# One DRAM array for q, k and v with two loads a tile, four attention tiles in memory, and four tiles' scores and values in the product banks

## The chip, the core and the metric

The kernel runs on one core of one Trainium2 chip. What counts is the device time of one execution in microseconds. The kernel before took 833.31 us in the median of three runs (833.04 to 835.87).

## The reference

Inputs are q, k and v of shape (4, 8, 576, 64) and the weights of two feed-forward layers. The attention is block-diagonal: each head's 576 tokens fall into nine chunks of 64, and a chunk attends only to itself. The result, as 2304 tokens by 512 features, passes two layers, 512 to 2048 to 512, everything in float32.

```python
scores = scale * np.matmul(q_c, k_c.transpose(0, 1, 2, 4, 3))   # chunks of 64 x 64
attn = softmax(scores)                                          # row maximum taken off first
out = np.matmul(attn, v_c)                                      # -> x: 2304 x 512
g = s * np.maximum(x @ w_in, 0.0) ** 2 + b                      # layer 1
x = g @ w_out
h = x @ w_in2                                                   # layer 2
g = np.maximum(h, 0.0) + np.log1p(np.exp(-np.abs(h)))
out = g @ w_out2
```

## The kernel before, in words

**Tiles.** Attention works in 18 tiles of 128 token rows by 512 columns. Two tiles, an even and an odd one, make a unit; three units make a group, the 384 columns of a large product. Every large product is made of three float32r matmuls of high and low parts, and each layer's first product goes by a seven-product (Strassen-like) scheme. So a finished tile is not merely copied: sums of its quarters are formed and each is split into a high and a low part (`even_forms`, `odd_forms`, with `split` at L505 and L514 and `sub` at L492).

**A tile's chain** (`attention`, L693). Scores on TensorE (PE) into a PSUM bank (L733); row maximum on VectorE (DVE, L747); for the first six tiles (`EARLY`) the maximum is scaled on DVE (L769) and ScalarE (ACT) takes eight exponentials that also sum (L757), for the others DVE subtracts (L779), ACT takes one exponential (L792) and DVE sums (L800); two small DVE operations give the reciprocal of the sum (L810, L811); POOL multiplies (L817); PE transposes (L833); ACT or DVE copies the transpose out (L350, L352); PE multiplies by v (L852, the values); then the forms. The chain's last PE step is called V, its scores sc, its transposes T, with the tile's number behind them: sc0, T0, V0 for the first tile.

**Memory and banks.** Tiles stand in three sets of places in memory, tile t in set t mod 3. Each has four loads: q (128 rows), two halves of k (64 rows each, to the two blocks of a zero-padded matrix) and v. q and k may be loaded again as soon as the scores of the set's old tile are through, v as soon as its values are. Scores, transposes and values share three PSUM banks `at`; five more, A (two) and S (three), belong to the large products. Each of the five is cleared once, at the very start, by a matmul of zeros (L1404).

**Weights.** The first layer's weights arrive as 8-byte numbers in loads of 512 KB and are converted by five DVE operations and one on ACT (`convert`: L400, L430, L444, L458, L472, and L417 on ACT). Then DVE, POOL and ACT form their sums and split them (`weights1`).

**The order.** `Work.order` is a planner that runs while the kernel is built: every piece of work has engines, an estimated cost, a due key, dependencies and places that it takes and gives back. It writes one fixed order for each engine; each engine then goes through its own list in that order, and an instruction that waits holds up all behind it. All loads and stores stand in one such list, that of SyncE (SP). Keys of the first tiles are `TILE0 + t * TILE1`, a tile's loads are due `LEAD_Q` earlier, and `W_KEY` gives the keys of the first two weight pieces.

Of the kernel before, what the change touches and what calls it, by code (L numbers as in the profile page):

```python
# [9 lines left out]
F32R = mybir.dt.float32r  # L10
# [8 lines left out]
P = 128  # L19
B, H, S, D = 4, 8, 576, 64  # L20
NT = B * S
DM = H * D
DFF = 2048
KK = DM // P
NP = H // 2
# [15 lines left out]

EARLY = 6


LEAD_F, LEAD_Q, LEAD_W, LEAD_G, LEAD_H, LEAD_X = 12.0, 12.0, 14.0, 10.0, 4.0, 16.0

TILE0, TILE1 = 0.0, 2.5
START = [28.0, 40.0, 56.0, 64.0, 84.0, 92.0, 100.0]
W_KEY = [1.0, 45.0]


A_AT = {4: 0, 1: 1, 2: 2, 5: 3, 6: 4, 7: 5, 3: 6}
# [4 lines left out]
XS = 2 * 7 * 2 * P  # L57
LAST = (NG - 1) * GROUP
AT_X2 = LAST * XS
AT_W1 = NU * XS  # L60
# [9 lines left out]
AT_T = AT_XO + NXO * DM  # L70
# [27 lines left out]
class Work:  # L98
# [31 lines left out]
    def order(self, places):  # L130
# [14 lines left out]
        def earliest(op, e):  # L145
            t = engine[e]
            for d in op.deps:
                t = max(t, d.end + (self.OTHER if d.on != e else 0 if e == "PE" else self.SAME))
            for d in op.after:
                t = max(t, d.start)  # L150
            for u in op.takes:
                t = max(t, min(free[u.kind].values(), default=float("inf")))
            return t

        for op in self.ops:
# [3 lines left out]
        while len(done) < len(self.ops):  # L159
# [10 lines left out]
            t, op, e = best  # L170
# [45 lines left out]
def block_attention_two_layers(  # L216
    ctx: ExitStack,
    tc: tile.TileContext,
    q: bass.AP,
    k: bass.AP,  # L220
    v: bass.AP,
    w1: bass.AP,
    w2: bass.AP,
    s: bass.AP,
# [465 lines left out]
    last_small = [[], [], [], []]  # L690
    held = {}

    def attention(t, key):  # L693
        u, odd = t // 2, t % 2
        a = AT_X2 + t % 3 * XS
        spans = {
            "q": (a, 512),
            "k": (a + 512, 1024),
            "aT": (a + 1536, 512),
            "v": (a + 2048, 512),  # L700
            "e": (a + 2560, 512),
        }
        of = lambda x: mem(*spans[x], 0)
        own = []
        sp = lambda *x: [spans[y] for y in x]
        loads = [
            load(key - LEAD_Q, lambda: of("q"), lambda: q[t], P * DM * 4, uses=own, w=sp("q"), after=turn.get("q", ()))
        ]
        turn["q"] = loads[:1]
        for hp in range(2):  # L710
            p0 = hp * D

            loads.append(
                load(
                    key - LEAD_Q,
                    lambda p0=p0, hp=hp: of("k")[p0 : p0 + D, hp * 512 : (hp + 1) * 512],
                    lambda p0=p0: k[t, p0 : p0 + D],
                    D * DM * 4,
                    after=loads[-1:],
                    w=[(spans["k"][0] + hp * 512, 512)],  # L720
                )
            )
        load_v = load(
            key - LEAD_Q + 0.5, lambda: of("v"), lambda: v[t], P * DM * 4, uses=own, w=sp("v"), after=loads[-1:]
        )
        sc, pt, px = Place("at"), Place("at"), Place("at")

        def scores(e):
            out_ = at(sc).rearrange("p (a b k) -> p a b k", a=NP, b=2)
            kb = of("k").rearrange("p (b a c k) -> p b a c k", b=2, a=NP, c=2)  # L730
# [10 lines left out]
        o1 = add({"PE": 1.07}, key, scores, loads, [sc], r=sp("q", "k"))  # L741
        mx, sm = small[t % 4] if tc else (None,) * 2
        heads = lambda x: x.rearrange("p (h k) -> p h k", h=H)
        o2 = add(
# [109 lines left out]
                        )  # L854

        key += 0.3
        o10 = add({"PE": 1.07}, key, values, [o9, load_v], [px], r=sp("aT", "v"))
        got = lambda: two(at(px))
        hold = u >= LAST
        if hold or not odd:  # L860
# [34 lines left out]
    def quad(ph, i, j, w, keys, kinds):  # L895
# [68 lines left out]
            hid_in.setdefault((ph, n, j), []).append(st)  # L964
            quads_done[ph].append(st)

        p1 = product(1, ba, free_from.get("s2", ()), True)
        sb = seed(bb, keys[6] - 1, [p1])
        p6 = product(6, ba, [sb])
        c2 = add(  # L970
# [171 lines left out]
    def second_by_blocks(ph, t0):  # L1142
# [166 lines left out]
                        )  # L1309

    scalars = [
        add({"SP": 0.63}, -3, lambda e: nc.sync.dma_start(out=s_sb, in_=s.to_broadcast([P, 1]))),
        add({"SP": 0.63}, -3, lambda e: nc.sync.dma_start(out=b_sb, in_=b.to_broadcast([P, 1]))),
    ]

    T = 6 * mm(N)
# [36 lines left out]
    times += [(t0, 1), (t0 + 7 * T, 1)]  # L1353
    for t in tiles:
        attention(t, x_key(t))
    another_use()
    for u in range(LAST, NU):
        forms_held(u, x_key(TILES - 1) + 3 + u - LAST)
# [34 lines left out]
    with tc.manual_schedule():  # L1393
        nc.scalar.preload_act_table_set("exp_and_others")
        make_identity(nc, ident)
        for x in range(AT_X2, AT_W1, XS):
            nc.gpsimd.memset(mem(x + 512, 512, 0)[D:P], 0.0)
            nc.gpsimd.memset(mem(x + 1024, 512, 0)[0:D], 0.0)

        zero, ones = mem(AT_T, 512), mem(0, 512).bitcast(F32R)  # L1400
        nc.vector.memset(zero, 0.0)
        nc.vector.tensor_copy(out=ones, in_=zero)
        for x in bank["A"] + bank["S"]:
            nc.tensor.matmul(x, ones[:, :P], ones, start=True, stop=True)  # L1404
        for op in done:
            op.emit(op.on)


_INS = ["q", "k", "v", "w1", "w2", "s", "b"]
_OUTS = [((DM, NT), "float32")]  # L1410


def _laid_out(q, k, v, moe_w_in, moe_w_out, moe_s, moe_b, moe2_w_in, moe2_w_out):
    import numpy as np

    nch = S // D

    def heads_on_rows(a):

        a = a.reshape(B, NP, 2, nch, D, D).transpose(0, 3, 2, 5, 1, 4)  # L1420
        a = a.reshape(TILES, 2, 2, D, NP, D).transpose(0, 2, 3, 4, 1, 5)
# [12 lines left out]
    return {  # L1434
        "q": heads_on_rows(q),
        "k": heads_on_rows(k),
        "v": tokens_on_rows(v),
        "w1": weights(moe_w_in, moe_w_out),
        "w2": weights(moe2_w_in, moe2_w_out),
        "s": moe_s,  # L1440
        "b": moe_b,
    }
# [30 lines left out]
```

## Time and profile before

| | |
|---|---|
| median of three runs | 833.31 us |
| the profiled execution | 836.06 us |
| its span, first to last instruction | 834.3 us |
| PE busy | 795.1 us (95%) |
| DVE busy | 654.0 us (78%) |
| ACT busy | 506.4 us (61%) |
| POOL busy | 148.6 us (18%) |
| DMA moved | 180.26 MB, mean 216 GB/s |

Shares of the whole span hide the stages. The first 100 us, where the attention runs, look quite different from the rest, so this profile is read by windows: how long each engine was busy in a stretch, and at which waits it stood still. A duration is that of a group of instructions that the trace merges: "x16" is one tile's scores, "x4" its transposes, "x32" one tile's values where the group ends within 2 us or less.

### The profile page before, as it was taken

The page shows a single profiled execution, that of the slowest core. Times are in us where ns is not written, and L with a number is a line of the kernel's source. Part 1 is how long each engine was busy: PE and PEld are TensorE (multiplying, and loading weights), DVE is VectorE, ACT ScalarE, POOL GpSimd, SP SyncE. Part 2 cuts the span into 40 slices and gives each one's busy share as a digit, 9 for nine tenths or more (in the row PEclk, how much of TensorE's full clock was granted, in tenths as well). Part 3 has the DMA queues.
Part 4 walks back from the last instruction along what each step waited for, and adds up shares of the span by engine and source line. Part 5 has one row for each costly group of instructions (what it writes and reads, how often), then busy time and mean ns, then how long its engine had stood idle before and what let it go on. Part 6 is the DMA issues. An engine that isn't in the chain of part 4 may idle for free.

```text
span 834.3 us, 14524 instructions
## 1 busy us (share of the span) xinstructions
PE 795.1 (95%) x5117; PEld 775.0 (93%) x5117; DVE 654.0 (78%) x1174; ACT 506.4 (61%) x1076; POOL 148.6 (18%) x162
## 2 busy tenths in 40 slices
PE   4688889999999999999999989999999999999998
PEld 3577789999998999999999989999999999999997
DVE  5799888888967869888888776778784767777865
ACT  3655555666656877767767655555555655555543
POOL 4254240111111003222213540111110000000000
PEclk9899999999999999999999999999999999999999
DMA  8665347868757835767662027657667996688851
GB/s 235 195 190 170 106 144 241 262 240 269 257 218 275 324 107 161 244 225 255 224 197 88 11 95 262 232 197 251 246 233 253 354 372 226 203 262 297 277 187 57
DMA packets 80632, 180.26 MB, mean 216 GB/s; under 512 B 9008, under 2 KB 53040, under 8 KB 79664
## 3 DMA queue, kind: packets, MB, share of 16 engines
q1 hardware_dynamic: 80560, 179.34, 63.9%
q8 instruction: 40, 0.66, 0.3%
q14 instruction: 32, 0.26, 0.1%
HBM read 111.15 MB, written 68.16 MB: 215 GB/s over the span
## 4 chain that ended last, share of the span: by engine, by line
PE 83%; DVE 8%; DMA 3%; ACT 3%; issue 1%; POOL 1%; SPq 0%; ACTq 0%; DVEq 0%
PE at L916 17%; PE S L916 10%; PE S L1093 9%; PE at L1093 9%; PE S L1244 8%; PE at L1244 8%; PE A L916 7%; PE A L1093 6%; PE A L1244 5%; DVE operands L514 2%; DVE mem L492 2%; PE at L852 2%; PE at L733 1%; DMA mem<-in_w_dram 1%; DMA last<-in_k_dram 1%
## 5 line engine op out<-in xcount | busy, mean ns | idle before, releaser
L492 POOL TENSOR_TENSOR mem<-mem 128x256 f32<-128x256 f32 x120 | 109.6, 923 | 414.1 <-DVE mem L472 309.2
L514 DVE TENSOR_TENSOR operands<-mem,operands 128x384 fp32r<-128x384 f32 (+4 forms) x186 | 130.9, 720 | 45.0 <-ACT operands L505 43.1
L505 ACT CAST operands<-mem 128x384 fp32r<-128x384 f32 (+4 forms) x186 | 112.3, 620 | 58.8 <-PE at L1244 36.1
L514 DVE TENSOR_TENSOR operands<-last,operands 128x384 fp32r<-128x384 f32 (+2 forms) x184 | 110.5, 616 | 42.4 <-ACT operands L505 39.9
L505 ACT CAST operands<-last 128x384 fp32r<-128x384 f32 (+2 forms) x184 | 94.3, 528 | 73.2 <-PE A L1093 46.5
L916 PE MATMUL at<-operands 128*128 128x384 f32 x624 | 122.4, 340 | 4.1 <-ACT mem L350 2.0
L916 PEld LDWEIGHTS at<-operands 128*128 128x128 f32 x624 | 110.4, 190 | 6.7 <-ACT mem L350 2.7
L1093 PE MATMUL S<-operands 128*128 128x384 f32 x432 | 90.7, 335 | 0.4 <-DVE operands L514 0.4
L1093 PE MATMUL at<-operands 128*128 128x384 f32 x432 | 90.3, 334 | 0.0
L1244 PE MATMUL S<-operands 128*128 128x384 f32 x384 | 87.4, 334 | 0.1
L1244 PE MATMUL at<-operands 128*128 128x384 f32 x384 | 87.1, 334 | 0.0
L916 PE MATMUL S<-operands 128*128 128x384 f32 x420 | 83.5, 337 | 0.9 <-DVE S L492 0.8
L1093 PEld LDWEIGHTS S<-operands 128*128 128x128 f32 x432 | 76.2, 188 | 0.9 <-DVE operands L514 0.6
L1093 PEld LDWEIGHTS at<-operands 128*128 128x128 f32 x432 | 76.2, 188 | 0.0
L948 ACT ACTIVATE mem<-S 128x384 f32<-128x384 f32 x104 | 50.6, 492 | 41.1 <-PE S L916 34.4
L916 PEld LDWEIGHTS S<-operands 128*128 128x128 f32 x420 | 73.5, 188 | 1.5 <-DVE S L492 1.3
L1244 PEld LDWEIGHTS S<-operands 128*128 128x128 f32 x384 | 68.3, 188 | 0.4 <-DVE operands L514 0.4
L1244 PEld LDWEIGHTS at<-operands 128*128 128x128 f32 x384 | 68.3, 188 | 0.0
L916 PE MATMUL at<-last,operands 128*128 128x384 f32 x336 | 67.2, 337 | 0.6 <-ACT S L938 0.2
L492 DVE TENSOR_TENSOR mem<-mem 128x384 f32<-128x384 f32 (+1 forms) x108 | 60.7, 589 | 9.1 <-ACT mem L948 7.8
L1093 PE MATMUL A<-operands 128*128 128x384 f32 x288 | 65.4, 334 | 0.0
L916 PE MATMUL A<-operands 128*128 128x384 f32 x300 | 60.5, 341 | 3.3 <-ACT S L938 1.5
(79 smaller groups left out, 1217.0 us busy)
## 6 DMA issues: line engine op xcount, KB each, us to landing
mem<-in_w_dram SPq DMA_DIRECT2D x64, 512.0 KB, 4.4
summed<-mem SPq DMA_DIRECT2D x168, 192.0 KB, 2.3
mem<-summed SPq DMA_DIRECT2D x30, 768.0 KB, 4.8
hid<-mem SPq DMA_DIRECT2D x96, 192.0 KB, 2.9
last<-hid SPq DMA_DIRECT2D x24, 768.0 KB, 5.3
last<-summed SPq DMA_DIRECT2D x12, 768.0 KB, 4.9
mem<-forms SPq DMA_DIRECT2D x7, 1024.0 KB, 7.1
last<-in_q_dram SPq DMA_DIRECT2D x18, 256.0 KB, 4.2
```

The source lines that it names most:

```text
L492: lambda e: on(e).tensor_tensor(out=out(), in0=x(), in1=y(), op=op or ALU.subtract),
L505: lambda e: nc.scalar.copy(out=hi().bitcast(F32R), in_=x()),
L514: lambda e: nc.vector.tensor_tensor(out=lo().bitcast(F32R), in0=x(), in1=hi(), op=ALU.subtract),
L733: nc.tensor.matmul(out_[c * D : (c + 1) * D, pr], of("q")[:, pr * P + c * D : pr * P + (c + 1) * D], kb[:, :, pr, c, :], start=True, stop= ...
L852: nc.tensor.matmul(at(px)[y, x], of("v")[y, x], of("aT")[y, x], start=True, stop=True)
L916: nc.tensor.matmul(acc(dst)().rearrange("p (u c) -> p u c", u=GROUP), l[a], r[c], start=start and kk == 0 and x == 0, stop=kk == 1 and x == 2,
L948: lambda e: nc.scalar.activation(out=at(go), in_=acc(place)(), func=AF.Softplus if ph else AF.Relu),
L1093: nc.tensor.matmul(at(accs[d])[:, :N], l[a], r[c], start=m == 0 and z == 0, stop=m == NM - 1 and z == 2,)
L1244: nc.tensor.matmul(at(accs[d])[:, :N], l[a], r[c], start=i == 0 and y == 0, stop=i == NF - 1 and y == 2,)
```

## The change

It has four parts.

1. q, k and v come from one DRAM array. A tile has two loads: rows 0 to 63 bring q, the first k block and v as one stretch of 1536 numbers a row, rows 64 to 127 bring the same three as 3 pieces of 512 numbers, because the second k block lies elsewhere in memory. Scores and values now both wait for both loads.
2. Tiles stand in four sets. The transposed exponentials (aT) take the place of q. Both loads of a tile wait until the values of the set's old tile are through.
3. The scores of tiles 0 to 3 go to the A banks and their values to the S banks. The five clearing matmuls move from the start to behind tile 3's last use of these banks (`prime`, L1368 of the changed kernel), and the large products wait for them.
4. Keys: the first weight piece is due at 6 instead of 1, the two loads of scalars s and b at 60 instead of -3. The planner counts several places of one kind that a piece of work takes together.

```diff
+EARLY_BANKS = 4
...
-W_KEY = [1.0, 45.0]
+W_KEY = [6.0, 45.0]
...
-        a = AT_X2 + t % 3 * XS
...
+        a = AT_X2 + t % 4 * 5 * DM
+        spans = {x: (a + y * DM, DM) for x, y in (("q", 0), ("k0", 1), ("v", 2), ("e", 3), ("k1", 4), ("aT", 0))}
...
-        loads = [
-            load(key - LEAD_Q, lambda: of("q"), lambda: q[t], P * DM * 4, uses=own, w=sp("q"), after=turn.get("q", ()))
-        ]
-        turn["q"] = loads[:1]
+        loads = []
         for hp in range(2):
-            p0 = hp * D
+
+            def three(hp=hp):
+                rows = mem(a, 5 * DM, 0)[hp * D : (hp + 1) * D].rearrange("p (n c) -> p n c", c=DM)
+                return rows[:, 0:5:2] if hp else rows[:, 0:3]
 
             loads.append(
                 load(
                     key - LEAD_Q,
-                    lambda p0=p0, hp=hp: of("k")[p0 : p0 + D, hp * 512 : (hp + 1) * 512],
-                    lambda p0=p0: k[t, p0 : p0 + D],
-                    D * DM * 4,
-                    after=loads[-1:],
...
+                    three,
+                    lambda hp=hp: qkv[t, hp * D : (hp + 1) * D],
+                    3 * D * DM * 4,
+                    after=loads[-1:] or turn.get("qkv", ()),
...
-        load_v = load(
-            key - LEAD_Q + 0.5, lambda: of("v"), lambda: v[t], P * DM * 4, uses=own, w=sp("v"), after=loads[-1:]
-        )
-        sc, pt, px = Place("at"), Place("at"), Place("at")
+        turn["qkv"] = loads[-1:]
+        sc, pt, px = Place("A" if t < EARLY_BANKS else "at"), Place("at"), Place("S" if t < EARLY_BANKS else "at")
...
-        o10 = add({"PE": 1.07}, key, values, [o9, load_v], [px], r=sp("aT", "v"))
+        o10 = add({"PE": 1.7}, key, values, [o9, *loads], [px], r=sp("aT", "v"))
+        if t < EARLY_BANKS:
+            early.extend([o1, o10])
...
-        p1 = product(1, ba, free_from.get("s2", ()), True)
+        p1 = product(1, ba, (*primed, *free_from.get("s2", ())), True)
...
-        add({"SP": 0.63}, -3, lambda e: nc.sync.dma_start(out=s_sb, in_=s.to_broadcast([P, 1]))),
-        add({"SP": 0.63}, -3, lambda e: nc.sync.dma_start(out=b_sb, in_=b.to_broadcast([P, 1]))),
+        add({"SP": 0.63}, 60, lambda e: nc.sync.dma_start(out=s_sb, in_=s.to_broadcast([P, 1]))),
+        add({"SP": 0.63}, 60, lambda e: nc.sync.dma_start(out=b_sb, in_=b.to_broadcast([P, 1]))),
...
+        if t == EARLY_BANKS - 1:
+
+            places = [Place(kind) for kind in "AASSS"]
+
+            def prime(e):
+                for p in places:
+                    nc.tensor.matmul(at(p), ones()[:, :P], ones(), start=True, stop=True)
+
+            primed.append(add({"PE": 1.2}, x_key(t) + 0.7, prime, early, places, r=[ONES]))
...
-        for x in range(AT_X2, AT_W1, XS):
-            nc.gpsimd.memset(mem(x + 512, 512, 0)[D:P], 0.0)
-            nc.gpsimd.memset(mem(x + 1024, 512, 0)[0:D], 0.0)
...
+        for x in range(AT_X2, AT_X2 + 4 * 5 * DM, 5 * DM):
+            nc.gpsimd.memset(mem(x + DM, DM, 0)[D:P], 0.0)
+            nc.gpsimd.memset(mem(x + 4 * DM, DM, 0)[0:D], 0.0)
...
-        for x in bank["A"] + bank["S"]:
-            nc.tensor.matmul(x, ones[:, :P], ones, start=True, stop=True)
...
+    q, k, v = heads_on_rows(q), heads_on_rows(k), tokens_on_rows(v)
+    qkv = np.stack([q, k, v], axis=2)
+    qkv[:, D:] = np.stack([q, v, k], axis=2)[:, D:]
```

**How the order moves.** SP's list began with tile 0's four loads, then two weight loads, then q, k, v of tile 1 and of tile 2. It now begins with the two loads of tiles 0, 1 and 2, then the two weight loads, then tile 3, then s and b, then tile 4.

The DVE list begins, before, with the following; L400 to L472 convert the first weight piece, L747 is the maximum of tile 0 and L810, L811 its reciprocal:

```order
L747 TENSOR_REDUCE mx_76<-at_70 128x8
L400 TENSOR_SCALAR mem<-mem 128x512
L769 TENSOR_SCALAR mx_76<-mx_76 128x8
L430 TENSOR_SCALAR mem<-mem 128x512
L444 SCALAR_TENSOR_TENSOR mem<-mem 128x512
L458 SCALAR_TENSOR_TENSOR mem<-mem 128x512
L472 SCALAR_TENSOR_TENSOR mem<-mem 128x512
L400 TENSOR_SCALAR mem<-mem 128x512
L430 TENSOR_SCALAR mem<-mem 128x512
L810 TENSOR_SCALAR sm_77<-sm_77 128x8
L811 RECIPROCAL sm_77<-sm_77 128x8
```

With the change it begins so (L751 is what L747 was, L402 what L400 was, L814 and L815 what L810 and L811 were):

```order
L751 TENSOR_REDUCE mx_76<-A_65 128x8
L773 TENSOR_SCALAR mx_76<-mx_76 128x8
L751 TENSOR_REDUCE mx_78<-A_66 128x8
L402 TENSOR_SCALAR mem<-mem 128x512
L814 TENSOR_SCALAR sm_77<-sm_77 128x8
L815 RECIPROCAL sm_77<-sm_77 128x8
L773 TENSOR_SCALAR mx_78<-mx_78 128x8
L432 TENSOR_SCALAR mem<-mem 128x512
```

The maxima of tiles 0 and 1 now stand ahead of the first weight conversion, which stands ahead of tile 0's reciprocal.

The PE list, before, behind the five clearing matmuls:

```order
L733 MATMUL at_70<-last_120 64x128 x8
L733 MATMUL at_71<-last_120 64x128 x8
L733 MATMUL at_72<-last_120 64x128 x8
L833 MATMUL at_70<-ident,last_120 128x128 x4
L852 MATMUL at_70<-last_120 64x64 x16
L733 MATMUL at_71<-last_120 64x128 x8
L733 MATMUL at_70<-last_120 64x128 x8
L833 MATMUL at_72<-ident,last_120 128x128 x4
L852 MATMUL at_72<-last_120 64x64 x16
```

And with the change, from its start (L737 are scores, L837 transposes, L856 values):

```order
L737 MATMUL A_65<-last_120 64x128 x8
L737 MATMUL A_66<-last_120 64x128 x8
L737 MATMUL A_65<-last_120 64x128 x8
L837 MATMUL at_70<-ident,last_120 128x128 x4
L737 MATMUL A_66<-last_120 64x128 x8
L856 MATMUL S_67<-last_120 64x64 x16
L837 MATMUL at_71<-ident,last_120 128x128 x4
L856 MATMUL S_68<-last_120 64x64 x16
L837 MATMUL at_72<-ident,last_120 128x128 x4
L737 MATMUL at_70<-last_120 64x128 x8
L856 MATMUL S_69<-last_120 64x64 x16
```

Tile 1's transposes and values now follow tile 0's at once; before, the scores of tiles 3 and 4 stood between.

The third place is the clearing's new one on PE, between the values of tile 4 and the transposes of tile 5; the scores in the last row are tile 7's:

```order
L856 MATMUL at_71<-last_120 64x64 x16
L1368 MATMUL A_65<-operands 128x512
L1368 MATMUL A_66<-operands 128x512
L1368 MATMUL S_68<-operands 128x512
L1368 MATMUL S_69<-operands 128x512
L1368 MATMUL S_67<-operands 128x512
L837 MATMUL at_70<-ident,last_120 128x128 x4
L737 MATMUL at_72<-last_120 64x128 x8
```

Thirteen large products of the first layer stand ahead of the last tile's values in both orders.

## Rows read from the trace of the kernel before

**Rows 1.** Windows: us, busy time (instructions) by engine, granted clock, DMA share, GB/s.

```profile
core 0: us, PE busy (x) PEld busy (x) DVE busy (x) ACT busy (x) POOL busy (x), PEclk, DMA share, GB/s
0.00:10.00 10.00, 4.47 (x21) 3.09 (x21) 3.87 (x8) 2.91 (x10) 4.02 (x12) 1.00 0.77 242
10.00:20.00 10.00, 5.00 (x36) 3.93 (x36) 7.86 (x15) 5.14 (x28) 4.34 (x5) 1.00 1.00 230
20.00:30.00 10.00, 7.64 (x100) 6.68 (x100) 5.42 (x14) 6.28 (x34) 2.10 (x2) 0.92 0.63 179
30.00:40.00 10.00, 5.20 (x78) 4.24 (x74) 8.39 (x16) 5.61 (x26) 3.51 (x4) 0.84 0.72 230
40.00:50.00 10.00, 8.66 (x122) 7.17 (x120) 8.46 (x17) 6.23 (x20) 3.47 (x4) 0.73 0.41 128
50.00:100.00 50.00, 43.32 (x658) 37.68 (x660) 46.37 (x91) 27.63 (x51) 22.26 (x23) 1.00 0.49 150
100.00:140.00 40.00, 36.96 (x220) 34.80 (x215) 35.85 (x59) 25.45 (x53) 9.44 (x10) 1.00 0.56 189
140.00:834.00 694.00, 683.83 (x3900) 677.43 (x3898) 537.80 (x959) 427.15 (x861) 99.47 (x102) 1.00 0.65 223
```

**Rows 2.** Waits of DVE from 0 to 100 us: total us, times, longest.

```profile
DVE mx L747 <- PE at L733: 7.5, 3, 5.1
DVE mem L492 <- PE at L852: 2.9, 2, 2.1
DVE mem L352 <- PE at L852: 2.0, 1, 2.0
```

**Rows 3.** Timeline of DVE: start, duration, instruction, idle time before it and its releaser.

```profile
7.32 0.69 DVE L747 TENSOR_REDUCE mx<-at 128x8 f32<-128x512 f32 x1 [5.14 <-PE at L733]
...
8.26 0.16 DVE L769 TENSOR_SCALAR mx<-mx 128x8 f32<-128x8 f32 x1
```

**Rows 4.** Timeline of PE in the first 101 us.

```profile
2.23 1.22 PE L1404 MATMUL A<-operands 128*128 128x512 f32 x2 [2.23 <-DVE operands L1402]
3.25 1.48 PE L1404 MATMUL S<-operands 128*128 128x512 f32 x3
5.31 1.97 PE L733 MATMUL at<-last 128*64 128x128 f32 x16 [0.57 <-DMA last<-in_k_dram]
12.46 1.98 PE L733 MATMUL at<-last 128*64 128x128 f32 x16 [5.18 <-DMA last<-in_k_dram]
...
17.76 1.12 PE L833 MATMUL at<-ident,last 128*128 128x128 f32 x4
20.08 1.97 PE L852 MATMUL at<-last 64*64 64x64 f32 x32 [1.20 <-DVE last L352]
...
48.81 0.63 PE L833 MATMUL at<-ident,last 128*128 128x128 f32 x4
50.12 1.15 PE L852 MATMUL at<-last 64*64 64x64 f32 x32 [0.67 <-ACT last L350]
...
99.39 1.15 PE L852 MATMUL at<-last 64*64 64x64 f32 x32
```

**Rows 5.** DMA traffic of 0:3, 3:6, 6:9, 9:12, 30:33 and 674:684 us.

```profile
DMA packets 171, 0.32 MB, mean 107 GB/s; under 512 B 15, under 2 KB 15, under 8 KB 171
DMA packets 377, 0.88 MB, mean 292 GB/s; under 512 B 49, under 2 KB 49, under 8 KB 377
DMA packets 379, 0.99 MB, mean 330 GB/s; under 512 B 51, under 2 KB 51, under 8 KB 379
DMA packets 396, 0.70 MB, mean 234 GB/s; under 512 B 54, under 2 KB 54, under 8 KB 396
DMA packets 338, 1.01 MB, mean 337 GB/s; under 512 B 39, under 2 KB 39, under 8 KB 338
DMA packets 742, 4.26 MB, mean 426 GB/s; under 512 B 80, under 2 KB 80, under 8 KB 647
```

**Rows 6.** DMA issues of 684:700 us: number, size, us to landing.

```profile
mem<-summed SPq DMA_DIRECT2D x4, 768.0 KB, 4.4
```

More of the change, by code (lines that the diff above doesn't have):

```diff
@@ L150, in earliest @@
                 t = max(t, d.start)
-            for u in op.takes:
-                t = max(t, min(free[u.kind].values(), default=float("inf")))
+            kinds = [u.kind for u in op.takes]
+            for z, kind in enumerate(kinds):
+                times, n = sorted(free[kind].values()), kinds[:z].count(kind)
+                t = max(t, times[n] if n < len(times) else float("inf"))
             return t
@@ L218, in block_attention_two_layers @@
     tc: tile.TileContext,
-    q: bass.AP,
-    k: bass.AP,
-    v: bass.AP,
+    qkv: bass.AP,
     w1: bass.AP,
@@ L691, in block_attention_two_layers @@
     held = {}
+    early, primed = [], []
+    ONES = (5 * XS, 512)
+    ones = lambda: mem(*ONES).bitcast(F32R)
     def attention(t, key):
         u, odd = t // 2, t % 2
-        a = AT_X2 + t % 3 * XS
[L696 to L702, printed above, removed]
+        a = AT_X2 + t % 4 * 5 * DM
+        spans = {x: (a + y * DM, DM) for x, y in (("q", 0), ("k0", 1), ("v", 2), ("e", 3), ("k1", 4), ("aT", 0))}
         of = lambda x: mem(*spans[x], 0)
@@ L715, in attention @@
                     key - LEAD_Q,
-                    lambda p0=p0, hp=hp: of("k")[p0 : p0 + D, hp * 512 : (hp + 1) * 512],
-                    lambda p0=p0: k[t, p0 : p0 + D],
-                    D * DM * 4,
-                    after=loads[-1:],
-                    w=[(spans["k"][0] + hp * 512, 512)],
-                )
-            )
-        load_v = load(
-            key - LEAD_Q + 0.5, lambda: of("v"), lambda: v[t], P * DM * 4, uses=own, w=sp("v"), after=loads[-1:]
-        )
-        sc, pt, px = Place("at"), Place("at"), Place("at")
+                    three,
+                    lambda hp=hp: qkv[t, hp * D : (hp + 1) * D],
+                    3 * D * DM * 4,
+                    after=loads[-1:] or turn.get("qkv", ()),
+                    w=[spans["k1"], (a, DM // 2), (a + 2 * DM, DM // 2)]
+                    if hp
+                    else [spans["k0"], (a + DM // 2, DM // 2), (a + 2 * DM + DM // 2, DM // 2)],
+                )
+            )
+        turn["qkv"] = loads[-1:]
+        sc, pt, px = Place("A" if t < EARLY_BANKS else "at"), Place("at"), Place("S" if t < EARLY_BANKS else "at")
         def scores(e):
             out_ = at(sc).rearrange("p (a b k) -> p a b k", a=NP, b=2)
-            kb = of("k").rearrange("p (b a c k) -> p b a c k", b=2, a=NP, c=2)
+            kb = mem(a + DM, 4 * DM, 0).rearrange("p (n a c k) -> p n a c k", n=4, a=NP, c=2)[:, 0:4:3]
             for pr in range(NP):
@@ L739, in scores @@
                     )
-        o1 = add({"PE": 1.07}, key, scores, loads, [sc], r=sp("q", "k"))
+        o1 = add({"PE": 1.7}, key, scores, loads, [sc], r=sp("q", "k0", "k1"))
         mx, sm = small[t % 4] if tc else (None,) * 2
@@ L1395, in block_attention_two_layers @@
         make_identity(nc, ident)
-        for x in range(AT_X2, AT_W1, XS):
-            nc.gpsimd.memset(mem(x + 512, 512, 0)[D:P], 0.0)
-            nc.gpsimd.memset(mem(x + 1024, 512, 0)[0:D], 0.0)
-        zero, ones = mem(AT_T, 512), mem(0, 512).bitcast(F32R)
+        for x in range(AT_X2, AT_X2 + 4 * 5 * DM, 5 * DM):
+            nc.gpsimd.memset(mem(x + DM, DM, 0)[D:P], 0.0)
+            nc.gpsimd.memset(mem(x + 4 * DM, DM, 0)[0:D], 0.0)
+        zero = mem(AT_T, 512)
         nc.vector.memset(zero, 0.0)
-        nc.vector.tensor_copy(out=ones, in_=zero)
-        for x in bank["A"] + bank["S"]:
-            nc.tensor.matmul(x, ones[:, :P], ones, start=True, stop=True)
+        nc.vector.tensor_copy(out=ones(), in_=zero)
         for op in done:
             op.emit(op.on)
-_INS = ["q", "k", "v", "w1", "w2", "s", "b"]
+_INS = ["qkv", "w1", "w2", "s", "b"]
 _OUTS = [((DM, NT), "float32")]
@@ L1434, in _laid_out @@
     return {
-        "q": heads_on_rows(q),
-        "k": heads_on_rows(k),
-        "v": tokens_on_rows(v),
+        "qkv": qkv,
         "w1": weights(moe_w_in, moe_w_out),
```

## The prediction

> **What bounds the kernel now.** I read the windows first [rows 1]. Behind 140 us PE is busy 683.83 of 694 us: there the time is the large products, which the change leaves alone. From 100 to 140 us PE stands 3.04 us. In the first 100 us it is busy only 4.47 + 5.00 + 7.64 + 5.20 + 8.66 + 43.32 = 74.3, so 25.7 us stand open, nearly all of what a change can win. What the products wait for there is the attention: its last values begin at 99.39 [rows 4]. And what sets the attention's pace is DVE. From 50 to 100 us DVE is busy 46.37 of 50; from 0 to 50 only 3.87 + 7.86 + 5.42 + 8.39 + 8.46 = 34.0, so it stands 16.0 us [rows 1]. The waits say for what [rows 2]: for scores 7.5 us, 5.1 of them once, at the start, and for values (L852) 2.9 and 2.0. Behind the scores stand the loads: PE stood 5.18 us until tile 1's k had landed at 12.46 [rows 4]. Meanwhile DVE converted weights, so it looks busy, while tile 1 had not begun. Then PE's list held V0 back until 20.08, and values five tiles on (V5) began at 50.12.
>
> So the measure is simple: DVE's work up to the attention's end is the same in both kernels (no DVE instruction is added or removed), and what its idle time shrinks by, the end comes earlier, if PE can follow. Half a per cent, about what a measurement can tell from no change, is 4.2 us.
>
> **The loads.** A tile is 2 x 64 rows x 6 KB = 0.786 MB. Rows of 2 KB moved at 234 GB/s (9 to 12 us: 342 packets above 512 B for 0.70 MB, 2 KB each), a mix of weight rows of 4 KB and v at 337, and rows of 6 to 8 KB at 426 [rows 5]. I take 426 for the first load of a tile, whose rows are 6 KB at both ends (0.92 us), and 234 for the second, whose rows fall into three pieces in memory (1.68): 2.6 us a tile; 512 KB of weights at 337, 1.56. How long after its last byte a load counts as landed: by the traffic summed up [rows 5], tile 0's q and k (0.524 MB) were through at 3.7 and its scores began at 5.31 [rows 4], 1.6 later; all up to tile 1's k (2.36 MB) at 9.7 and its scores at 12.46, 2.7 later. These are my two ends.
>
> With 1.6: by 3.0 us 0.32 MB have moved, as before; tile 0 is through at 4.85 and lands at 6.45, 1.1 later than now since it holds v too; tile 1 lands at 9.05 (now 12.46), tile 2 at 11.65, the first weights at 13.2, tile 3 behind the second weights at 17.4. With 2.7, those behind tile 0 land 1.1 later.
>
> [...]
>
> **DVE's idle time after the change, up to V5.**
> - Start, until the clearing source is written: 0.9, as before.
> - Until tile 0's maximum: scores take 1.97 [rows 4], so 6.45 + 1.97 = 8.42; DVE is free at 7.32 - 5.14 = 2.2 [rows 3], so 6.25. Now it is 5.14: 1.1 worse.
> - Until tile 1's maximum: tile 0's takes 0.69 and the scaling 0.16 [rows 3], DVE is free at 9.3; tile 1's scores run 9.05 to 11.0: 1.75, new. Weight conversion filled this time before.
> - The conversion's first operation then stands ahead of tile 0's reciprocal and waits for the weights, 11.75 to 13.2: 1.45, new.
> - From there DVE has several tiles' work in its list. V0 stands behind tile 3's scores: 17.4 + 1.97 = 19.4 (now 20.08). Behind V0 come T1 and the copy of its result, for which DVE waits about 0.45, and one gap of 0.1, if PE's steps behind V1 go at the pace they had at 48 us and later: transposes 0.63, values 1.15 [rows 4]. That is 0.55. The waits of 2.0, 2.0 and 2.1 for scores and values [rows 2] go, since tiles 1 to 3 have their exponentials before V0 is through, and V1 follows V0 at once.
>
> Sum 10.9, against 16.0 now. Ahead of V5 both lists hold about the same work for DVE (two weight conversions and most of a third, the forms of tiles 0 to 4, the maxima of a few tiles more), 34 us; so V5 is 5.1 us ahead. With 2.7 for landing, tile 1's wait is 2.85 and the sum 12.0: 4.0 ahead. I take the middle, **4.5**.
>
> **The other edits.** The five clearing matmuls cost 1.22 + 1.48 = 2.7 [rows 4] where PE waited for tile 0 anyway, so taking them away there wins nothing. At their new place, with PE at the later pace, about half of that, 1.35, stand between V4 and T5. Tile 5's multiply on POOL is due some 0.7 us after V4, so PE is 0.65 late, and DVE has tile 5's and tile 6's rows to go on with: nothing. At the slow pace 2.7: 2.0 late, and tile 7's maximum, for which PE must first do T5, finds DVE empty for about 1.7. The first product waits for the clearing too, but it began at 57 and the clearing is done by about 45: nothing. 36 loads fewer: SP issues them while it waits for PE, nothing. The keys of s and b move little: they still stand right behind tile 3. Two more memsets on POOL end about 1.1 us later, ahead of any work there. The first weights' conversion ends some 5 us later, and nothing needs them before 57.
>
> **Does the lead last?** From 50 to 100 us DVE is busy 93% [rows 1], and V5 to V17 takes 49.3 us [rows 4], 4.1 a tile. Nothing in that stretch waits for what the change takes away, so the lead passes to the last values, now at 99.39, then near 95, and, as the products ahead of it are as many, to the end. The products' own waits may move by a us either way, as every list behind is written anew.
>
> Sum: the profiled execution took 836.06 us (span 834.3, 1.8 around it), the median is 2.75 lower. 836.06 - 4.5 = 831.6 as this execution counts, and 833.31 - 4.5 = **828.8** against the median.
>
> **Rivals.**
> 1. *The lead melts on PE's pace.* From 5 to 22 us a tile's scores or values took 1.97 us, at 50 us and later values 1.15; the granted clock was 0.73 to 0.92 from 20 to 50 us and 1.00 later [rows 1, 4] (the slow early rows stand under a recorded 1.00, so I go by durations). If PE stays slow up to V5, the copies that wait for T1, V2, T3 and T4 stand 2.1 us instead of 0.55, and the clearing costs its 1.7: the lead is 4.5 - 3.25 = 1.25, 832.1. Against it: with the change PE's steps from tile 3's scores on lie close together, where now it stands 5 of the 10 us from 30 to 40. Chance 0.3.
> 2. *Slower: the sets of memory bind.* A tile's loads now wait for the values four tiles back, where q and k waited only for scores three back. The new list puts a tile's scores mostly one values-step, 4.1 us, and one transpose, 0.63, behind the values that free its set. A load of 768 KB in gaps landed 4.4 us after its issue [rows 6], and there is a second issue: about 4.9, against 4.7. That is a tie, which DVE's list covers. If tiles land at 5.5, each of the twelve from 6 to 17 stands 0.8 us, 9.6 in all, and the time is 833.31 - 4.5 + 9.6 = 838.4. It turns the sign from 5.1 us (12 x 0.4). For it speaks that weights and stores share the DMA engines; against it that they are 0.49 busy from 50 to 100 us [rows 1]. Chance 0.12.
> 3. *More.* If the second load too runs at 426 GB/s, a tile takes 1.85 us, tile 1 lands 1.5 and the weights 2.25 earlier; the third and fourth item shrink by about 2.2: 826.6. Chance 0.12.
>
> The forecast itself has 0.46.
>
> **The numbers.** The forecast reaches from 4.0 to 5.1 us of lead, and with a us for the products' waits from 3.0 to 6.1: 827.2 to 830.3. The range takes in rival 3 and rival 1 with a little over a us beyond each: 825.3 to 833.5; it leaves out rival 2. Faster by over half a per cent (below 829.1): rival 3 and 0.38 of the forecast, 0.50. Within it: rival 1 and 0.08, 0.38. Slower: 0.12.
>
> **What would show it.** Right: tile 0's scores at 6.5, tile 1's near 9.6, V0 near 19.5, V5 near 45.6, the last values near 95; DVE idle in the first 45 us about 11.5. Wrong: DVE waiting for scores with a tile's load as the cause behind 50 us (rival 2); scores and values still at 1.97 between 25 and 45 us (rival 1); V5 ahead but the last values not, which would break the step that the lead lasts.

## The result, and the profile after

The changed kernel takes **844.33 us** in the median of four runs (841.48 to 844.87), the kernel before 834.09 in the same comparison (833.04 to 835.87): ratio 1.0124, interval 1.0095 to 1.0153. I had forecast 828.8, at most 833.5. It is some 10 us slower, and outside the range. The profiled spans are 843.0 and 834.3 us, so 8.7 us of it can be read in the two traces. The ratios of the runs below leave out one execution of run 2, which took 1576 us where its other nine took 833 to 838.

The windows of the changed kernel, columns as in [rows 1]:

```profile
0.00:10.00 10.00, 1.98 (x16) 1.60 (x16) 2.07 (x4) 1.28 (x1) 5.05 (x14) 1.00 0.82 184
10.00:20.00 10.00, 5.07 (x36) 3.92 (x36) 5.39 (x12) 6.38 (x35) 1.93 (x2) 1.00 0.94 235
20.00:30.00 10.00, 6.27 (x88) 5.24 (x88) 9.71 (x19) 5.78 (x24) 5.72 (x7) 1.00 0.48 114
...
50.00:100.00 50.00, 40.23 (x612) 33.85 (x608) 47.53 (x91) 28.33 (x50) 23.70 (x25) 1.00 0.75 183
100.00:140.00 40.00, 36.97 (x249) 34.69 (x250) 27.30 (x48) 24.74 (x50) 7.62 (x9) 0.96 0.44 143
140.00:834.00 694.00, 686.42 (x3910) 679.15 (x3909) 535.83 (x955) 433.53 (x872) 94.61 (x102) 1.00 0.65 225
```

The first 10 us already differ: DMA is as busy as before (0.82 against 0.77) but moves 184 GB/s instead of 242. And from 50 to 100 us DVE is busy for 47.53 us against 46.37, yet PE for 40.23 against 43.32: DVE works more, and PE gets less from it.

The PE timeline of the changed kernel shows where the attention stands (L737 scores, L837 transposes, L856 values):

```profile
7.10 1.98 PE L737 MATMUL A<-last 128*64 128x128 f32 x16 [7.10 <-DMA last<-in_qkv_dram]
10.68 1.98 PE L737 MATMUL A<-last 128*64 128x128 f32 x16 [1.60 <-DMA last<-in_qkv_dram]
14.26 1.98 PE L737 MATMUL A<-last 128*64 128x128 f32 x16 [1.60 <-DMA last<-in_qkv_dram]
...
20.26 1.98 PE L737 MATMUL A<-last 128*64 128x128 f32 x16 [1.88 <-DVE sm L814]
22.16 1.97 PE L856 MATMUL S<-last 64*64 64x64 f32 x32
...
31.30 1.97 PE L856 MATMUL S<-last 64*64 64x64 f32 x32
...
40.69 1.58 PE L737 MATMUL at<-last 128*64 128x128 f32 x16 [3.12 <-DMA last<-in_qkv_dram]
42.20 1.12 PE L837 MATMUL at<-ident,last 128*128 128x128 f32 x4
...
49.77 1.15 PE L856 MATMUL at<-last 64*64 64x64 f32 x32
...
105.68 1.15 PE L856 MATMUL at<-last 64*64 64x64 f32 x32
```

Tiles come 3.58 us apart (7.10, 10.68, 14.26), not the 2.6 of my sum. V0 begins at 22.16 (before 20.08 [rows 4], forecast 19.5), V5 at 49.77 (50.12, forecast 45.6), the last values at 105.68 (99.39, forecast near 95). The lead of 4.5 us never came about, and from V5 to V17 another 6.6 us were lost, in a stretch that I had said the change leaves alone.

DVE's ledger up to V17, which was the measure of the prediction, by windows that end at V17; first the kernel before, then the changed one (the columns are the stretch, its length, DVE's busy time and instructions, granted clock, DMA share, GB/s):

```profile
0.00:99.39 99.39, 80.37 (x157) 0.95 0.60 177
```

```profile
0.00:49.77 49.77, 33.99 (x67) 0.90 0.75 182
0.00:105.68 105.68, 84.50 (x164) 0.95 0.72 175
```

So V17 is 6.3 us later because DVE had 84.50 - 80.37 = **4.1 us more work** ahead of it, and stood 21.2 us instead of 19.0, **2.2 us more**. Up to V5 it stood 49.77 - 33.99 = 15.8 us, where I had 10.9 and the kernel before has 16.0. So the longer wait lies behind V5: 5.4 us there against 3.0. More than half of it is for ACT's activation of a finished product (L954), which must be through before DVE's next sum:

```profile
DVE S L494 <- ACT mem L954: 3.0, 2, 2.4
```

The work that was added shows in the operations on DVE up to V17, here the subtraction and sum of the weight conversion in the changed kernel (L446, L460 and L474 are L444, L458 and L472 of before):

```profile
L460 DVE SCALAR_TENSOR_TENSOR mem<-mem 128x512 uint32<-128x512 uint32 x6 | 7.1, 1187 | 0.0
L474 DVE SCALAR_TENSOR_TENSOR mem<-mem 128x512 f32<-128x512 f32 x6 | 5.2, 872 | 0.1
L446 DVE SCALAR_TENSOR_TENSOR mem<-mem 128x512 f32<-128x512 uint32 x6 | 4.6, 759 | 0.0
```

Six conversions stand ahead of the last values. In the kernel before the same three lines read x4:

```profile
L458 DVE SCALAR_TENSOR_TENSOR mem<-mem 128x512 uint32<-128x512 uint32 x4 | 4.5, 1116 | 0.0
```

The two new ones convert the third weight unit (at 76.56 and from 86.34 us), which the kernel before does from 112.36 us on, when the attention is over. With their two other operations (L402 and L432) the six conversions take 22.7 us of DVE, the four before 15.2: 7.5 us more. Part of this is made up: of the 18 copies of transposes ahead of V17, DVE had nine before and has four now, and ACT does the others. First before, then changed:

```profile
L352 DVE COPY last<-at 128x512 f32<-128x512 f32 x9 | 6.2, 686 | 1.5 <-PE at L833 1.2 <-ACT S L938 0.3
```

```profile
L354 DVE COPY last<-at 128x512 f32<-128x512 f32 x4 | 2.7, 684 | 1.9 <-PE at L837 1.9
```

So 7.5 us came and 3.5 went, which is the 4.1 but for a tenth.

In this execution 2.4 us are lost behind V17 (737.3 us to the end against 734.9). PE waits twice near 115 us, and then twelve matmuls take 3.83 us:

```profile
114.35 1.31 PE L922 MATMUL S<-operands 128*128 128x384 f32 x6 [1.07 <-ACT S L944]
116.42 3.83 PE L922 MATMUL A<-operands 128*128 128x384 f32 x12 [0.76 <-DVE mem L494]
```

From 140 to 260 us PE stands 2.4 us against 0.7 before. Neither can be put down to the change: run 5 has the lists of the changed kernel without these slow matmuls, and run 9 has the lists of the kernel before and stands 2.3 us from 140 to 260.

### The profile page after: what moved, and what is told of

Its sections match the earlier page's. It is cut to its first block, busy times and chain, and to the rows that moved or that the text cites. A ratio compares the mean times of both kernels' runs of the same rounds, so it can differ in the third digit from the quotient of the medians.

```text
span 843.0 us, 14444 instructions
## 1 busy us (share of the span) xinstructions
PE 797.3 (95%) x5117; PEld 775.9 (92%) x5117; DVE 647.4 (77%) x1162; ACT 514.1 (61%) x1088; POOL 146.3 (17%) x164
## 4 chain that ended last, share of the span: by engine, by line
PE 72%; DVE 3%; ACT 2%; DMA 1%; POOL 1%; issue 1%; ACTq 0%
PE at L922 16%; PE S L1099 9%; PE at L1099 9%; PE S L1250 8%; PE at L1250 8%; PE S L922 7%; PE A L1099 6%; PE A L1250 5%; PE A L922 4%; DMA summed<-mem 1%; DVE operands L516 1%; DVE mem L494 1%; ACT mem L954 1%; POOL mem L494 1%; POOL last L494 0%
## 5 line engine op out<-in xcount | busy, mean ns | idle before, releaser
L954 ACT ACTIVATE mem<-S 128x384 f32<-128x384 f32 x104 | 50.9, 491 | 39.0 <-PE S L922 31.1
L1099 PE MATMUL A<-operands 128*128 128x384 f32 x288 | 65.4, 334 | 0.0
L922 PE MATMUL A<-operands 128*128 128x384 f32 x300 | 62.8, 349 | 1.3 <-DVE mem L494 0.9
```

The source lines that it names most:

```text
L922: nc.tensor.matmul(acc(dst)().rearrange("p (u c) -> p u c", u=GROUP), l[a], r[c], start=start and kk == 0 and x == 0, stop=kk == 1 and x == 2,
L954: lambda e: nc.scalar.activation(out=at(go), in_=acc(place)(), func=AF.Softplus if ph else AF.Relu),
L1099: nc.tensor.matmul(at(accs[d])[:, :N], l[a], r[c], start=m == 0 and z == 0, stop=m == NM - 1 and z == 2,)
```

## The experiments

My theory after reading this had two causes: the loads of 64 rows are slow, and with them the chain "load waits for the values four tiles back" starves the first 50 us; and the planner, given other times, put two weight conversions ahead of the last tiles. The rival was that the conversions alone, or the banks, explain it. Each run is compared with the kernel before on the same chip.

**1. The third weight unit held.** Everything as changed, but the third unit's weight loads wait for the last tile's values:

```diff
-        c1 = convert(ph, 2 * i + 1, 0, key, lambda: at(wf)[:, :DM], [wf])
+        gone = [values_of[TILES - 1]] if ph == 0 and i == 2 else ()
+        c1 = convert(ph, 2 * i + 1, 0, key, lambda: at(wf)[:, :DM], [wf], gone=gone)
```

(and the same for `c0`).

> The changed kernel, with the loads of the third weight unit (two pieces) made to wait for the last tile's values, so that DVE's list holds four conversions ahead of the last tile instead of six. Theory 'weights ahead' (the two conversions that moved ahead of the last tiles, 7.35 us on DVE from 76 to 98 us, are what the stretch from V5 to V17 lost): V17 begins near 98.5 instead of 105.7, and the time is 837 (835 to 839). Theory 'loads late' (tiles arrive late because their loads wait for the values four tiles back and are slow): V17 stays at 104 or later, since DVE then only waits where it converted, and the time is 842 or more.

838.65 us, ratio 1.0067 (1.0043 to 1.0091): about 5 us come back. But V17 is at 104.10, only 1.6 earlier. The window up to V17 in this run says why:

```profile
0.00:104.10 104.10, 79.77 (x156) 0.93 0.69 167
```

DVE's work ahead of V17 fell by 4.7 us, but DVE now stands 24.3 us instead of 21.2: behind V5 it waits for the results of two large products (2.5 us, in the changed kernel 0.2) and for scores and transposes (2.2 against 0.4). The rest of the gain, 4.4 of the 6.0 us between the two spans (843.0 and 837.0), lies behind V17 by these two profiles; the stretch of slow matmuls near 116 us is gone there (granted clock from 100 to 140 us 1.00, in the changed kernel 0.96). Run 5 shows that this split depends on which execution is taken. My expected time was right, my expected V17 was not.

**2. One load of 128 rows a tile.** q, both k blocks with their zeros, and v come as one load of 8 KB a row: a third more bytes, no memsets on POOL. The planner was free to write new lists.

```diff
+            load(key - LEAD_Q, lambda: mem(a, 4 * DM, 0), lambda: qkv[t], 4 * P * DM * 4, ...
...
+    k0[:, :D], k1[:, D:] = k[:, :D], k[:, D:]
+    qkv = np.concatenate([q, k0, k1, v], axis=2)
```

> The changed kernel, with one load a tile of 128 rows by 8 KB: q, k0, k1, v with the zeros of the two k blocks from DRAM (1.05 MB instead of 0.79) and no clearing of k on POOL. If a load of 64 rows moves at half the rate because of its 64 rows, the first tiles' scores follow each other by about 2.5 us instead of 3.6 in spite of a third more bytes. If not, by 3.6 or more. The order still has six conversions ahead of the last tile: by 'weights ahead' the time is 841 or more; by 'loads late' it falls to 838 or less.

836.0 us, 1.0032 (1.0012 to 1.0053). Tiles 0 and 1 have their scores at 5.58 and 8.06, 2.48 us apart in spite of a third more bytes (3.58 in the changed kernel, 2.5 expected if 64 rows move at half the rate), V0 at 14.82 and V5 at 43.87; yet V17 is at 104.95. The time is what 'loads late' expected (838 or less). Its list has the six conversions ahead of V17 too, and 20 large products instead of 13. So this V17 can't be set against the others: PE has done 81.4 us of work up to it, 73.7 before, and 729 us follow it, not 735. The early stage is 6 us ahead and the time is still not below that of the kernel before. DVE's 86.3 us of work ahead of V17, against 80.4, agree with the second cause but do not show it by themselves.

**3. Banks alone.** The kernel before with the scores and values of four tiles in A and S and the clearing moved; loads, sets and keys as before.

```diff
+        sc, pt, px = Place("A" if t < EARLY_BANKS else "at"), Place("at"), Place("S" if t < EARLY_BANKS else "at")
```

> The kernel before with one part of the change: scores and values of tiles 0 to 3 in the A and S banks, the clearing matmuls behind tile 3, the planner's counting of several places. Loads, sets and keys as before; DVE's list has four conversions ahead of the last tile. By 'weights ahead' and by 'loads late' alike this is not slower: 830 to 836. If it is 839 or more, the banks or the clearing's new place cost, and both theories miss it.

837.02 us, 1.0083 (1.0041 to 1.0125): a miss. V5 at 42.94 looked like a lead of 7 us, V17 at 99.49 like none. Five conversions and 15 products stand ahead of V17 here, and PE stands 4.4 us for DVE's sums behind it. Even this one part brought a new list, and with that list it is slower than the kernel before.

**4. The change without the banks.** The clearing goes back to the start.

```diff
-        sc, pt, px = Place("A" if t < EARLY_BANKS else "at"), Place("at"), Place("S" if t < EARLY_BANKS else "at")
+        sc, pt, px = Place("at"), Place("at"), Place("at")
```

> The changed kernel without the banks: scores and values of all tiles in the three attention banks, clearing at the start; the new loads, four sets and keys stay. The order has six conversions ahead of the last tile. Both theories put the loss into what stays: 842 or more. If it falls to 838 or less, the banks are the cause.

846.58 us, 1.0169 (1.0139 to 1.0199), V17 at 116.40, with 20 products ahead of it. The banks are not what makes the change slow; without them it is about 4 us slower still, though the lists differ and the two intervals overlap.

**5. Rows of 6 KB in both loads.** The places of a tile are ordered k0, q, v, k1, so that rows 64 to 127 are one stretch too. The lists of all engines are those of the changed kernel.

```diff
-                return rows[:, 0:5:2] if hp else rows[:, 0:3]
+                return mem(a + hp * DM, 3 * DM, 0)[hp * D : (hp + 1) * D]
```

> The changed kernel with the places of a tile laid out as k0, q, v, k1, so that both loads of 64 rows are one stretch of 6 KB a row at both ends; the orders of all engines are the changed kernel's. If a load of 64 rows moves at half the rate because it fills only half the rows, the first tiles' scores still follow each other by about 3.6 us (0.79 MB at 220 GB/s) and the time stays at 842 to 846. If the 2 KB pieces of the second load were what slowed, they follow by 1.9 to 2.2 us and the time falls below 840.

843.96 us, 1.0122 (1.0092 to 1.0152): nothing. Scores at 6.92, 10.37 and 13.71. The 2-KB pieces were not it.

Since its lists are the changed kernel's, this run also shows what in one profile belongs to the one execution. V17 is at 107.82, not 105.68, and 734.1 us follow it, not 737.3 (before 734.9). DVE has 84.35 us of work up to V17, as there. Against this run, the span of run 1 is 4.9 us shorter, 3.7 of it ahead of V17. PE stands before the same matmuls near 116 us for as long as in the changed kernel, and the twelve behind take 2.38 us under a granted clock of 1.00, not 3.83:

```profile
116.48 1.34 PE L921 MATMUL S<-operands 128*128 128x384 f32 x6 [1.06 <-ACT S L943]
118.55 2.38 PE L921 MATMUL A<-operands 128*128 128x384 f32 x12 [0.73 <-DVE mem L494]
```

**6. The same lists, one load of 128 rows.** Of the two steps that issue a tile's loads one now issues the load of run 2, the other nothing; all orders on PE, DVE and ACT are those of the changed kernel. As in run 2, a third more bytes move and POOL has no memsets.

```diff
+            def whole(e, hp=hp):
+                if hp == 0:
+                    nc.sync.dma_start(out=mem(a, 4 * DM, 0), in_=qkv[t])
```

> The changed kernel's orders on PE, DVE and ACT, row by row, with one load a tile of 128 rows by 8 KB (1.05 MB, zeros included) in place of the first of its two and nothing in place of the second. Only the speed of loads differs, six conversions still stand ahead of the last tile. 'Loads late': V5 begins 4 us or more earlier than 49.8, and the time falls from 844 to 839 or less. 'Weights ahead' alone: V5 may come earlier, but DVE has the same work ahead of the last tile, so the time stays at 841 or more.

839.0 us, 1.0066 (1.0041 to 1.0091): the loads alone, with every order kept, are worth 5 us. The traffic from 4 to 10 us, while only tiles and the first weights are on their way, in the changed kernel, in run 5 and in this one:

```profile
DMA packets 493, 1.35 MB, mean 226 GB/s; under 512 B 48, under 2 KB 48, under 8 KB 493
```

```profile
DMA packets 276, 1.38 MB, mean 230 GB/s; under 512 B 51, under 2 KB 51, under 8 KB 276
```

```profile
DMA packets 355, 2.50 MB, mean 416 GB/s; under 512 B 43, under 2 KB 43, under 8 KB 57
```

With 64 rows 226 and 230 GB/s, whether a packet is 2 or 6 KB; with 128 rows 416. And in the changed kernel itself, from 14 to 15 us, when weight loads of 128 rows and 4 KB run:

```profile
DMA packets 115, 0.41 MB, mean 406 GB/s; under 512 B 16, under 2 KB 16, under 8 KB 115
```

In these four stretches the DMA share is 1.06, 1.02, 1.00 and 1.01, so here a busy DMA says nothing of the rate. Run 6 is also a test of my ledger with the loads as fast as I had thought, up to V5 and V17:

```profile
0.00:44.05 44.05, 33.83 (x65) 0.96 0.69 259
0.00:99.62 99.62, 84.87 (x164) 0.97 0.64 233
```

DVE stands 10.2 us up to V5 (I had 10.9), and V5 comes at 44.05 (I had 45.6). Item by item: 0.9 at the start (0.9), 7.3 for the first two maxima (8.0), 1.0 for the weights (1.45), 0.4 behind (0.55), and short gaps. It stands 14.8 us up to V17 against 19.0 before: of the 5.8 us less at V5, 4.3 are left. But 84.87 - 80.37 = 4.5 us more work eat it all, and V17 is back at 99.62. What its span has over that of the kernel before (837.3 against 834.3) lies behind V17 in this execution, with twelve matmuls in 3.91 us at 110.

**7. Both causes removed:** one load of 128 rows, and the third weight unit held; the edits of runs 1 and 2 together.

> The changed kernel with both: one load a tile of 128 rows, and the third weight unit behind the last tile's values. If slow loads and conversions ahead are the whole loss, it is faster than the kernel before: 829 (826 to 832), the lead that the prediction forecast. If 834 or more, a third cause is left (banks and clearing, or the order behind the attention).

**829.61 us** in 12 runs (828.29 to 832.26), ratio 0.9963 (0.9945 to 0.9981): faster than both kernels. The windows:

```profile
50.00:100.00 50.00, 46.42 (x630) 39.72 (x631) 39.98 (x80) 27.84 (x51) 20.17 (x20) 0.97 0.56 197
100.00:140.00 40.00, 37.35 (x208) 35.43 (x207) 35.23 (x61) 25.73 (x53) 8.92 (x10) 1.00 0.61 197
140.00:260.00 120.00, 119.41 (x683) 118.45 (x683) 100.97 (x168) 74.66 (x147) 21.40 (x24) 1.00 0.76 248
```

PE gets 46.42 us of work from 50 to 100 us (before 43.32, changed 40.23). The granted clock is 1.00 from 100 us on. PE stands 0.6 us from 140 to 260, not 2.4, but run 9 shows that this stretch differs by as much between two executions of the same lists.

**8. Run 7 without the banks:** the edits of runs 1, 2 and 4 together.

> As the run with one load of 128 rows and the held third weight unit, but without the banks: scores and values of all tiles in the three attention banks, clearing at the start. If the banks are worth what they were made for, it is 2 us or more slower than that run; if the banks cost, as the run with the banks alone (837.0) may mean, it is faster, 828 or less.

832.11 us in 12 runs, 0.9989 (0.9971 to 1.0008): 2.5 us more than run 7. With fast loads and no banks nothing is won. Its profile is of an execution of 834.44 us, 2.3 above the median.

**9. The kernel before, with the condition of run 1.** The edit of run 1; it changes no list there.

> The kernel before with the same single extra condition: the loads of the third weight unit wait for the last tile's values. Before already converts that unit only from 112 us, behind the attention. Theory (a new order of DVE's list took the time in the changed kernel, and the condition only undoes it): nothing to undo here, the ratio to before within 0.997 and 1.003, about 833. Rival (the condition is a gain of its own in any version, and the 829.6 of the version with both repairs owes its lead to it): 830 or less.

833.7 us, 1.0015 (0.9998 to 1.0032). The condition is no gain of its own. The run also shows how far one profile stands for a kernel: with the same lists V5 is at 48.11 here and at 50.12 in [rows 4], V17 at 97.38 and 99.39, and from 140 to 260 us PE stands 2.3 here and 0.7 there. A single time point carries some 2 us.

**10. Banks alone, with that condition:** the edits of runs 3 and 1 together.

> The kernel before with the banks alone (its own loads, three sets), and the third weight unit's loads held until the last tile's values. Without the condition that version had the fifth tile's values at 42.9 us, 7 earlier than before, yet its last values at 99.5 and 837.0 us, with five weight conversions and 15 products ahead of them. Theory (the lead was spent on a conversion moved forward and on PE standing for results behind it): the last values at 97 or earlier and 829 to 832.5 us. Rival (the lead is lost to something else, such as the pace of PE or the two products moved ahead): last values near 99 and 835 or more.

834.16 us, 1.0022 (1.0002 to 1.0041), V17 at 101.85. Neither: against run 3 it wins 3 us, so the fifth conversion probably did cost (the two intervals just touch); but no gain over the kernel before appears. Tile 1's scores begin at 12.60 here and at 11.15 in run 3, with the same loads, so part of run 3's lead at V5 probably was chance. Banks without early tiles bring nothing (run 10), early tiles without banks bring nothing (run 8), both together 3 us (run 7), each with lists of its own.

The runs that separate the two causes, side by side:

| a tile's loads | third unit | banks | run | ratio | V5 | V17 | products ahead of V17 |
|---|---|---|---|---|---|---|---|
| 2 x 64 rows | free | yes | changed | 1.0124 | 49.77 | 105.68 | 13 |
| 2 x 64 rows, same lists | free | yes | 5 | 1.0122 | 47.66 | 107.82 | 13 |
| 2 x 64 rows | held | yes | 1 | 1.0067 | 48.20 | 104.10 | 13 |
| 1 x 128, same lists | free | yes | 6 | 1.0066 | 44.05 | 99.62 | 13 |
| 1 x 128, new lists | free | yes | 2 | 1.0032 | 43.87 | 104.95 | 20 |
| 1 x 128, new lists | held | yes | 7 | 0.9963 | 43.72 | 97.87 | 14 |
| 1 x 128, new lists | held | no | 8 | 0.9989 | 42.57 | 100.98 | 17 |

Holding is worth 0.0057 with loads of 64 rows and 0.0069 with loads of 128, 5 to 6 us; loads of 128 rows are worth 0.0058 with the same lists, and 0.0092 and 0.0104 with new ones, 5 to 9 us. Taking both away turns a loss of 1.24% into a gain of 0.37%. With the lists kept only the loads were changed (run 6); holding the unit wrote new lists in runs 1 and 7, so that step stands for the conversions and for whatever the planner moved with them.

## Why the prediction was wrong, point by point

**What bounds the kernel: right.** DVE sets the attention's pace, and the attention's end and the products' start set the time. The ledger of DVE's idle time was a good instrument: where the loads come as fast as I had put them, in run 6, it gives 10.9 for a measured 10.2, and each item is near.

**"The loads": wrong, the term of 2.6 us a tile.** It measured 3.58. I had taken 426 GB/s for the first load because its rows are 6 KB, and 234 for the second because its pieces are 2 KB. Apart, in the changed kernel, they run at the same rate; from 9 to 10 us, when nearly all packets are first loads of 6 KB, and from 11 to 12 us, when they are second loads of 2 KB:

```profile
DMA packets 49, 0.23 MB, mean 229 GB/s; under 512 B 7, under 2 KB 7, under 8 KB 49
```

```profile
DMA packets 112, 0.23 MB, mean 227 GB/s; under 512 B 3, under 2 KB 3, under 8 KB 112
```

So the length of the pieces is not what decides, as run 5 shows too; what all the loads near 226 GB/s have in common is the 64 rows. The 234 GB/s of 9 to 12 us [rows 5] came from a stretch in which halves of k, 64 rows each, were under way together with loads of 128 rows, and I put the mixed rate down to the length of the rows. The microsecond before, 8 to 9 us, speaks against it; the traffic of the kernel before there:

```profile
DMA packets 185, 0.36 MB, mean 356 GB/s; under 512 B 26, under 2 KB 26, under 8 KB 185
```

The 159 larger packets carry 0.36 MB, 2.3 KB each, so nearly all are pieces of 2 KB, at 356 GB/s.

Sorted by rows, the rates agree: 226 and 230 GB/s with 64 (the changed kernel and run 5, 4 to 10 us), 406 and 416 with 128 (the changed kernel, 14 to 15 us, and run 6, 4 to 10 us). Why 64 rows move at little more than half the rate, no run shows. One load of 128 rows in place of the two, with the lists kept, is worth 5 us (run 6).

**The ledger up to V5: wrong by what follows from that.** The waits of DVE up to V5 in the changed kernel:

```profile
DVE mx L751 <- PE A L737: 9.6, 2, 6.9
DVE last L354 <- PE at L837: 1.9, 1, 1.9
DVE mem L402 <- DMA mem<-in_w_dram: 1.8, 1, 1.8
DVE mem L1415 <- PEq L1467: 0.9, 1, 0.9
DVE mem L354 <- PE S L856: 0.8, 1, 0.8
```

The first, third and fourth are my items 6.25 + 1.75, 1.45 and 0.9, in all 12.3 instead of 10.35. The two others, 2.7 where I had 0.55, stand behind loads that the sets held back, below. With 0.8 of short gaps that makes 15.8, and the lead is 0.3 us instead of 4.5.

**Rival 1, PE's pace: seen in part, but not what decided.** V1 and V3 took 1.15 us under a granted clock of 1.00, V2 and V4 1.97 under 0.50. So PE was slow at times up to V5, and V2's pace is a part of the 0.8. But the longest wait behind V0, the 1.9, stands behind a load, and run 6 reached V5 at 44.05 with V0, V1 and V4 slow too (1.97, 1.98 and 1.74 us).

**Rival 2, the sets of memory: partly right, and earlier than I looked.** I priced it at tiles 6 to 17 behind 50 us. There DVE hardly waits for scores, 0.4 us from 50 to 100 us. It binds at the sets' first turn. SP's own timeline in the changed kernel (start, duration):

```profile
10.56 0.48 SPq L1319 DMA_DIRECT2D b_sb<-in_b_dram  x1
24.22 3.62 SPq L369 DMA_DIRECT2D last<-in_qkv_dram  x4
27.89 1.06 SPq L369 DMA_DIRECT2D mem<-in_w_dram  x2
33.30 5.42 SPq L369 DMA_DIRECT2D last<-in_qkv_dram  x4
```

From 11 to 24 us SP issues nothing: tile 4's loads wait for V0, which ends at 24.1. Tile 6's wait for V2, which ends at 33.3, and land at 40.69, 7.4 us later, behind two weight loads and at 201 GB/s (36 to 39 us). PE stands 3.12 us for them with T4 behind in its list, and DVE the 1.9 for T4's copy. Tile 4's scores came 0.97 us late in the same way, with V2 behind them and DVE's 0.8 for its result. The point from which this rival decides was 5.1 us; I had taken 4.9 from a load of 768 KB over 128 rows [rows 6].

**"DVE's work up to the attention's end is the same in both kernels": wrong, and it could be read beforehand.** No instruction was added, but two conversions, 7.5 us of DVE's time, moved ahead of V17. Nor did DVE keep all it had: five copies, 3.5 us, went to ACT. The sum is 4.1 us more. In the orders I had compared only the first 50 us and the count of large products. I had not counted what else stands ahead of the last values. By this step alone 828.8 would have become 833.

**"Does the lead last?": most of the idle time did, the time did not.** Run 6 keeps 4.3 us less idle up to V17, of 5.8 us less up to V5; the 1.5 between go to a wait for ACT's L953 (2.4 us), like that for L954 in the changed kernel. What undoes the rest is the added work. That behind V17 "the products' own waits may move by a us" was too small for one execution: with the changed kernel's lists 737.3, 734.1 and 737.7 us follow V17 (changed, runs 5 and 6), with those of before 734.9 and 735.1 (before, run 9).

**The other edits: about right.** The clearing at 46 us took 2.3 us and no DVE wait stands behind it. The banks were worth some 4 us in the changed kernel (run 4), and 2.5 in run 7, by versions with other lists.

What stays open: how much of the second cause is the conversions themselves. In run 1 the hold takes 7.0 us of conversion off DVE ahead of V17 and gives it two copies back, 4.7 us less in sum, and the time falls by 5; but V17 moved by only 1.6 us against the changed kernel and 3.7 against run 5, and no run moved the conversions with all else in place. The slow matmuls near 116 us are not their doing: in run 5 they are gone with the conversions where they were, and the time is the changed kernel's. Nor was a version tried that keeps three sets with loads of 128 rows.

## What to carry to other kernels

Read the rate of a load off a stretch in which only loads of its shape run, and ask what all of them have in common: rows, pieces and size, not the first property that fits. Where a planner writes the order, count the work of the bounding engine ahead of the end that matters in both lists, all of it, before pricing any wait. Before a stretch of one trace is put down to a change, see how it looks in a second execution of the same lists. And when a change with several parts comes out slower, look for the part that spoils it: here one load in place of two, and one condition, made it faster than both.

## What the runs showed of the hardware

- Loads into 64 rows moved 226 to 230 GB/s with the DMA share at 1.01 to 1.06, in packets of 2 KB (227 from 11 to 12 us of the changed kernel) and of 6 KB (230 from 4 to 10 us of run 5) alike; loads into 128 rows moved 406 GB/s in packets of 4 KB (14 to 15 us of the changed kernel, share 1.01) and 416 in packets of 8 KB (4 to 10 us of run 6, share 1.00).
- In the changed kernel PE stood 1.07 and 0.76 us within some 3 us, and the twelve matmuls of 384 columns behind took 3.83 us; the granted clock of 115 to 120 us is 0.66 in the mean, and 0.50 from 116.3 to 119.6 us. Run 6 shows the same (1.06 and 0.76, then 3.91 with 0.66 from 110 to 115 us). In run 5, with the same lists, PE stood 1.06 and 0.73 us and the twelve took 2.38 us under 1.00. So these waits alone do not bring the slow stretch.
- V1 and V3 of the changed kernel took 1.15 us under a granted clock of 1.00, V2 and V4 1.97 under 0.50. V0 took 1.97 too, from 22.16. The windows up to there show 1.00, but the first entry of the clock in that trace is at 24.1 us (before: 24.9), so a 1.00 ahead of it is no reading, in [rows 1] and in the prediction either.
